# Projections and first layer in 64x32 tiles, scores and P V as separate visits, and a new order

## The chip, the cores and the metric

The kernel runs on one core of a Trainium2 chip. Its time is device microseconds of one execution; the median of several runs counts, and a profile shows one execution instruction by instruction. The core has TensorE (PE, matmuls; the loading of its stationary operand is listed apart as PEld), VectorE (DVE), ScalarE (ACT), GpSimd (POOL) and SyncE (SP), which here issues DMAs. [...]

## The reference

x is 2048 tokens by 448, bfloat16. Two branches start from its layer norm, and the result joins them:

```python
xn = _layernorm(x, axis=-1)
s = _A_ref(xn, A_wqkv, A_wo)
g = _silu(_B_ref(xn, B_w1, B_b1, B_w2, B_b2))
return x + s * g
```

Branch A is local attention with 16 heads of 28: every token attends to 8 keys, itself and those 2, 4, ... 14 tokens back.

```python
q, k, v = qkv[0], qkv[1], qkv[2]          # from xn @ wqkv
idx = pos[:, None] - off[None, :]         # off = 0, 2, ..., 14
logits = jnp.where(mask, einsum(q, kg) * Dh ** -0.5, -1e9)
o = einsum(softmax(logits), vg)           # then o @ wo
```

Branch B is a dense network: `gelu(xn @ w1 + b1) @ w2 + b2`, with w1 448 x 1792 and w2 1792 x 448.

## The kernel before

Tokens are put in the order "even ones first, then odd ones", so that the 8 keys of a token are 8 neighbours. There are 16 tiles of 128 tokens, in four chunks of 512, and nine attention blocks of 4 x 57 tokens (the fifth 4 x 56).

**Order.** Every piece of work is a task with engine, estimated cost, dependencies, buffers it takes and gives, and a priority (tables `PRIO` and `LATER`). `_Plan.run` plays the tasks through in time: of those that could start within `SLACK` (0.12 us) of the earliest on that engine, it takes the one of highest priority, with a bonus (`SAME` 20) for a TensorE task in the tile shape ("mode") that TensorE is in, and `TILED` 30 while it is in a small shape. A change of mode is booked at `SWITCH` 0.095 us. `emit` then issues all instructions in the order of planned starts, so each engine's program is fixed.

**TensorE's work.** The projections (`qk_rows` L532, `vproj` L556) and the first layer (`ff1` L591) have a contraction of 448 = 7 x 64. `pair` takes two such jobs, a and b, with a bank each: in four steps the upper 64 rows of the array serve a and the lower 64 serve b, then in three steps the other way round, so that all seven 64-row pieces of both are done in seven steps of two concurrent matmuls of 64x128 (`together`). Between the two parts a `nop` on GpSimd or SP waits for the last two matmuls of the first, and the first two of the second wait for the `nop` (`behind`), so that the two halves of the array never write one bank at once. `first_batch` does the first two tiles' projections in 128x128, with a last step in halves.

The second layer (`ff2_part` L627, 14 matmuls a tile) and the output projection (`final_part` L796, 4 a tile) use the whole array, 128x128. Scores (`scores_of` L677) use 32x64 tiles, 64 matmuls of 57 columns into four banks; P V (`values_of` L709) uses 64x32 tiles, 64 matmuls of 57 columns into two banks. `attn` makes visits of them: `VISITS` puts the scores of the first two blocks alone, then P V of block i together with the scores of block i+2 as one task.

**Other engines.** After scores, ScalarE takes the exponential of each of four banks (L687), and VectorE or GpSimd multiplies it by a 0/1 mask (L693; `MASK_ON` lets the planner choose, at 0.4 or 1.2 us). After P V, VectorE transposes, takes reciprocals, transposes back and scales (`output_of`, L719, L723, L728, L733). ScalarE does the GELU (L595) and the tanh of the second layer (L655); VectorE adds b2 (L649, y), forms g (L659), multiplies with the output projection (L801, sg) and adds x (L807, o; for the first eight tiles GpSimd may do it), and SP stores the tile (L811). The last tile is done in two halves of 224 columns. GpSimd's queue also issues the copies of v into windows (`dma_sb`, L354), and SP's the transposes of xn and of q, k (`dma_T`, L360) and the loads (L347). Exponentials and GELU are kept in stages (`STAGES`): GELU of chunks 0 and 1, exponentials of blocks 0 to 5, GELU of chunk 2, exponentials of blocks 6 to 8, GELU of chunk 3.

Of the kernel before, what the change touches and what calls it, by code (L numbers as in the profile page):

```python
# [17 lines left out]
TILED = 30  # L18
SAME = 20
HOPS = ("POOL", ("SP", "POOL"))  # L20
MASK_ON = (("DVE", "POOL"), (0.4, 1.2))


def VISITS(bs):
    out = [[("S", b)] for b in bs[:2]]
    for i, b in enumerate(bs):
        out.append([("P", b)] + [("S", c) for c in bs[i + 2:i + 3]])
    return out
# [11 lines left out]
class _Task:  # L40
    __slots__ = ("eng", "cost", "deps", "fn", "prio", "take", "give", "slots",
                 "start", "end", "on", "ndep", "users", "tail", "seq", "table", "limit", "mode", "out")


class _Plan:
# [7 lines left out]
    def add(self, eng, cost, fn, deps=(), prio=0, take=(), give=(), tail=0.0, table=(), limit=None,  # L53
            mode=128):
# [5 lines left out]
        t.mode, t.out = mode, None  # L60
# [14 lines left out]
    def _at(self, t, e, free):  # L75
        at = free.get(e, 0.0)
        for p, n in t.take.items():
            if len(p.free) < n or p.fifo and p.fifo[0] is not t:
                return None
            at = max(at, sorted(p.free)[n - 1][0] + HOP)  # L80
        if t.table and self.table not in t.table:
            at += TABLE
        for d in t.deps:
            at = max(at, d.end - d.tail if d.on == e else d.end + HOP)
        if e == "PE" and t.mode != self.mode:
            at = max(at, free.get(e, 0.0) + SWITCH)
        return at

    def run(self):
# [6 lines left out]
        self.mode = 128  # L96
        ready = [t for t in self.tasks if not t.ndep]
        order = []
        while ready:
# [14 lines left out]
            tiled = first[2] == "PE" and self.mode < 64  # L114
            at, t, e, c = min(near, key=lambda k: (-k[1].prio - (TILED if tiled and k[1].mode < 64 else SAME if k[2] == "PE" and k[1].mode == self.mode else 0),
# [4 lines left out]
            if e == "PE" and t.fn is not None:  # L120
                self.mode = t.out or t.mode
# [43 lines left out]
def kernel(  # L165
# [80 lines left out]
    def ring(name, n, shape, dt=BF16, fifo=False):  # L246
# [24 lines left out]
        "project": (49.5, 205, 104, 52.5,),  # L271
        "project2": (147, 150, 101, 61,),
        "values": (89.5, 62.5, 21, 58,),
        "attn": (185, 179.5, 78, 174.5, 106.5, 106, 138.5, 136.5, 32.5,),
        "ff1": (185, 180, 84.5, 176.5, 66.5, 64.5, 156.5, 189.5, 203, 146, 76, 114.5, 77.5, 179.5,
            75.5, 118.5, 180.5, 14.5, 163, 68, 151, 115.5, 194.5, 167.5, 180, 188.5, 86, 93,),
        "gelu": (62.5, 22.5, 95, 92.5,),
        "ff2": (144, 162.5, 103.5, 142.5, 44.5, 112.5, 67, 5, 89, 106.5, 101.5, 75, 74, 55, 11.5,
            6.5,),
        "final": (140, 19.5, 70.5, 47, 112, 34.5, 23.5, 142.5, 73, 53, 198.5, 188.5, 81.5, 126.5,  # L280
            180, 71,),
        "norm": (37.5, 132, 179.5, 129.5, 74.5, 99, 161, 69, 63, 62, 43.5, 73, -5.5, 90, 133.5,
            150,),
        "loads": (166.5, 166, 188, 139.5, 54.5,),
        "stats": (47.5, -60, 180.5, 23, 127, 56, 188.5, 77, 197.5, -13.5, 185, 205.5, 138, 14, 52.5,
            138.5,),
        "turn_x": (108.5, -1, 28, 116, 210, 116.5, 131.5, 160, 41.5, 79.5, 70, 119, -4.5, 74.5,
            132.5, 111,),
        "turn_qk": (68.5, 112, 174.5, 90, 80, 6, 149.5, 60.5, 4, 140.5, 199.5, 96.5, 103, 166.5,
            140, 156,),  # L290
        "move_v": (81.5, 95, 23, 95, 18.5, 26.5, 8, 128, 29.5,),
        "copies": (50, 119.5, 58.5, 76, 32.5, 135.5, 43, 1, 87, 79.5, 129, 77, 32, 41.5, 135,),
    }
    LATER = {"swap": 135, "qk": 165, "v": 29.5, "gelu": 30.5, "exp": 55.5, "mask": -60, "pv": 45, "recip": -16.5, "os": 54.5, "y": 153.5, "tanh": 182.5, "g": 58, "sg": 183, "o": 120.5}
# [50 lines left out]
    def dma(eng, dst, src, kb, prio, deps=(), issue=0.5, rate=350.0):  # L345
        def fn(_):
            {"SP": nc.sync, "ACT": nc.scalar, "POOL": nc.gpsimd}[eng].dma_start(dst, src)  # L347
        a = plan.add(eng, issue, fn, [t_on] + list(deps), prio)
        return plan.add("DMA", kb / rate, lambda _: None, [a], prio, tail=1.7)
# [16 lines left out]
    def load_x(t0, n, prio, eng="SP", deps=()):  # L366
        d = dma(eng, x_sb[:, t0:t0 + n, :],
                rows(x_half, t0 * P, n * P).rearrange("(t p) d -> p t d", p=P), 112 * n, prio, deps,
                rate=270.0 if t0 < TPC else 350.0)
# [11 lines left out]
    def load_w(kt, prio):  # L381
        t_w.append([dma("SP", w_in[:, kt, :], A_wqkv[kt * P:(kt + 1) * P, :], 336, prio, rate=270.0)])
# [6 lines left out]
    t_w.append([dma("SP", w_in3[:64], tails[:, 0:3:2, :], 112, PRIO["loads"][3], rate=270.0),  # L389
                dma("SP", w_in3[64:], tails[:, 1:3, :], 112, PRIO["loads"][3], rate=270.0)])  # L390
# [78 lines left out]

    def together(top, bottom):  # L470
        return [(f(), g()) for f, g in zip(top, bottom, strict=True)]
# [5 lines left out]
    def pair(a, b, prio, early=False):  # L477
# [11 lines left out]
        def f2(k):  # L489
            held["told"] = (nc.gpsimd if k.on == "POOL" else nc.sync).nop()  # L490
            for i in held["last"]:
                behind(held["told"], i)
        told = plan.add(HOPS[0] if early else HOPS[1], 0.06, f2, [t], 300)

        def f3(k):
            p, q = buf(p_b, t, 0), buf(p_b, t, 1)
            for i in together([part(b, q, kt, 0, kt + 4) for kt in range(3)], [part(a, p, kt, 1, kt + 4) for kt in range(3)])[0]:
                behind(i, held["told"])
# [5 lines left out]
    def first_batch(tiles, prio, tiles0=0):  # L504

        f = []
        for kt in range(3):
            for i, js in enumerate(tiles):
                def f1(k, kt=kt, i=i, js=js):
                    for q, j in enumerate(js):  # L510
                        j.part(buf(p_b, f[i] if kt else k, q), kt, 2, kt == 0, False)
# [14 lines left out]
    def qk_rows(t, which, prio):  # L526
        cs = slice(t * P, (t + 1) * P)

        def part(ps, kt, half, start, stop):
            r = half_rows(half)  # L530
            w = w_in[r, kt, which * D:(which + 1) * D] if kt < 3 else w_in3[r, 0, :]
            return nc.tensor.matmul(ps[:, :D], xnT[r, kt, cs], w, start=start, stop=stop)  # L532

        def evac(a, own, i):
# [6 lines left out]
            if len(t_row[t]) == 2:  # L541
                t_qk[t] = dma_T(qkT[:, :, :, cs].rearrange("p w g c -> p (w g) c"), lambda: b[:].rearrange("p w h c -> p (w h c)"),
                                t_row[t], PRIO["turn_qk"][t], None, 2, 1.9 if t < 3 else 3.8 if t == TPC else 2.0 if t == TPC + 1 else 1.27)
# [6 lines left out]
    def vproj(t, prio):  # L550
        k0 = t * P

        def part(ps, kt, half, start, stop):
            r = half_rows(half)
            w = w_in[r, kt, 2 * D:] if kt < 3 else w_in3[r, 1, :]
            return nc.tensor.matmul(ps[:, :D], xnT[r, kt, k0:k0 + P], w, start=start, stop=stop)  # L556
# [7 lines left out]
    def values(b):  # L564

        t_v[b], v_at[b] = [], []
        for i in range(2):
            first = None
            for w in range(2):
                k0 = VIS[b][2][w][i][1]  # L570
                for lo in sorted({k0, max(k0, (k0 + NK - 1) // P * P)}):
# [6 lines left out]
                    t_v[b].append(d)  # L578
# [6 lines left out]
    def ff1(c, mt, prio, gate):  # L585
# [3 lines left out]
        def part(ps, kt, half, start, stop):  # L589
            r = half_rows(half)  # L590
            return nc.tensor.matmul(ps[:], w1[r, kt, ms], xnT[r, kt, cs], start=start, stop=stop)  # L591
# [74 lines left out]
    def scores_of(b):  # L666
        q, nq, wins = VIS[b]

        def fn(banks):
            for i in range(2):  # L670
                for g in range(G):
                    for hl in range(4):
                        for w in range(2):
                            r = slice(32 * hl, 32 * hl + 32)
                            q0, k0 = wins[w][i]
                            c0 = (G * i + g) * nq
                            nc.tensor.matmul(banks[hl][NK * w:NK * w + NK, c0:c0 + nq], qkT[r, 1, g, k0:k0 + NK],  # L677
                                             qkT[r, 0, g, q0:q0 + nq], start=True, stop=True)
        return fn, [t_qk[t] for t in range(wins[0][0][1] // P, (q + 4 * nq - 1) // P + 1)]

    def weights_of(b, a, at, prio, gate):
# [3 lines left out]
        for hl in range(4):  # L685
            def f2(k, hl=hl):
                nc.scalar.activation(buf(p_E, k)[:, :n], buf(p_b, a, at + hl)[:, :n], ACT.Exp, scale=SCALE)  # L687
            e = plan.add("ACT", act(n), f2, [a] + gate, prio + LATER["exp"], take=(p_E,), give=((p_b, a, at + hl),), table=("exp",))
# [8 lines left out]
    def values_of(b, exps):  # L697
        nq = VIS[b][1]

        def fn(banks):  # L700
            for hl in range(4):
                E = buf(p_E, exps[hl])
                for i in range(2):
                    v = buf(*v_at[b][i])
                    for g in range(G):
                        for w in range(2):
                            r = slice(NK * w, NK * w + NK)
                            c0, c1 = (2 * hl + i) * nq, (G * i + g) * nq
                            nc.tensor.matmul(banks[w][32 * g:32 * g + 32, c0:c0 + nq], v[r, 4 * g + hl, :],  # L709
                                             E[r, c1:c1 + nq], start=True, stop=True)  # L710
        return fn, tuple((p_E, e, 0) for e in exps) + tuple(v_at[b])

    def output_of(b, po, i, w, prio):
# [4 lines left out]
        def f5(k):  # L718
            nc.vector.transpose(buf(p_dt, k)[:, :32 * m], buf(p_b, po, i)[:, :32 * m])  # L719
        d = plan.add("DVE", dve(32 * m), f5, [po], prio + LATER["recip"], take=(p_dt,))  # L720
# [11 lines left out]
        def f8(_):  # L732
            nc.vector.tensor_tensor(out=oT[:, :, q0:q0 + 2 * nq],  # L733
                                    in0=buf(p_b, po, i)[:, :n].rearrange("p (l q) -> p l q", l=4),
                                    in1=buf(p_dt, d)[:, :n].rearrange("p (l q) -> p l q", l=4), op=ALU.mult)
        o = plan.add("DVE", dve(n), f8, [rb], prio + LATER["os"], give=((p_b, po, i), (p_dt, d, 0)))
# [3 lines left out]
    last_visit = {"S": [], "P": []}  # L740
    state = {}

    def attn(b, what):

        deps, take, give, fns, cost = [], [], (), [], -SWITCH
        for n, (w, blk) in enumerate(what):
            if not n or what[n - 1][0] != w:
                cost += SWITCH
            cost += 0.215
            if not n:  # L750
                cost += 0.03
            at = len(take)
            if w == "S":
                fn, d = scores_of(blk)
                d = d + state["early"]
                take += [p_b] * 4
                fns.append(lambda k, fn=fn, at=at: fn([buf(p_b, k, at + i) for i in range(4)]))
            else:
                exps, masked = state[blk]
# [207 lines left out]
```

## Time and profile before

| what | value |
|---|---|
| median of 3 runs (lowest, highest) | 157.52 us (157.37, 158.0) |
| profiled execution: time; span of its instructions | 157.98 us; 156.2 us |
| L591, first layer: matmuls, busy | 392, 44.7 us |
| L532 and L556, projections | 318, 24.3 and 13.4 us |
| L627, second layer | 238, 45.2 us |
| L796, output projection | 68, 14.1 us |
| L677 and L709, scores and P V | 576 each, 6.9 and 6.2 us |
| L693, masks on GpSimd; on VectorE | 28, 30.8 us; 8, 3.0 us |
| PE instruction blocks fetched (queue q8) | 17, 0.28 MB |

"Busy" is the union of a group's spans. Matmuls overlap, so a group's busy time is not their number times their mean length, and the modelled end of a matmul lies some 0.15 us behind the moment when the next can begin. A place where TensorE's work passes from one line to another is best read in the chain of waits, which gives each microsecond to one line.

### The profile page before, as it was taken

What the parts mean: (1) busy time and instruction counts of PE and PEld (TensorE: products, weight loads), DVE (VectorE), ACT (ScalarE), POOL (GpSimd) and SP (SyncE); (2) the same over time, 40 slices, a digit from 0 to 9 for tenths busy, and PEclk for the clock granted to TensorE, in tenths of its full rate; (3) what the DMA queues carried; (4) which work ended last, traced back from release to release, by engine and by line L of the source; (5) the groups of instructions that cost most, each with busy time, mean ns of one, the idle gap of its engine ahead of it and who ended that gap; (6) DMA issues with size and microseconds to landing.
All of it is one profiled execution on the core that took longest, in us unless ns stands there. A gap on an engine that the chain in (4) does not pass through costs nothing.

```text
span 156.2 us, 5305 instructions
## 1 busy us (share of the span) xinstructions
PE 150.1 (96%) x2204; PEld 77.8 (50%) x2204; DVE 113.2 (72%) x259; ACT 83.3 (53%) x149; POOL 74.7 (48%) x123
## 2 busy tenths in 40 slices
PE   6999999999999999999999999999999999999980
PEld 2544454444455555455554644455556444545570
DVE  4789551486266758997799895109899996998992
ACT  3245867378889416444634149782496587051220
POOL 7854856000459408839261098389599780000000
PEclk9999999999999999999999999999999999999999
DMA  4999969999749443099039822123300100200211
GB/s 156 329 317 315 167 124 187 237 269 307 141 95 166 64 82 90 10 192 138 4 83 85 131 70 73 38 76 83 105 0 4 34 31 29 63 4 0 68 36 43
DMA packets 33575, 17.36 MB, mean 111 GB/s; under 512 B 25331, under 2 KB 32387, under 8 KB 33552
## 3 DMA queue, kind: packets, MB, share of 16 engines
q1 hardware_dynamic: 31472, 14.03, 41.3%
q0 software_dynamic: 1936, 2.88, 8.5%
q8 instruction: 17, 0.28, 0.8%
q10 hardware_dynamic: 144, 0.11, 0.2%
q14 instruction: 6, 0.05, 0.1%
HBM read 7.06 MB, written 1.84 MB: 57 GB/s over the span
## 4 chain that ended last, share of the span: by engine, by line
PE 80%; DVE 8%; DMA 3%; POOL 2%; issue 2%; ACT 1%; SPq 1%; DVEq 0%; ACTq 0%; POOLq 0%
PE bank L627 23%; PE bank L591 22%; PE bank L532 11%; PE bank L796 7%; PE bank L556 6%; PE bank L677 4%; PE bank L709 4%; PE bank L327 3%; DMA xnT<-xn 3%; POOL v L354 2%; DVE sg L801 2%; DVE o L807 1%; DVE w_in L659 1%; ACT E L687 1%; DVE xn L438 1%
## 5 line engine op out<-in xcount | busy, mean ns | idle before, releaser
L627 PE MATMUL bank<-w,h 128*128 128x448 bf16 (+1 forms) x238 | 45.2, 342 | 0.0
L591 PE MATMUL bank<-xnT,w 64*128 64x512 bf16 x392 | 44.7, 376 | 0.0
L595 ACT ACTIVATE h<-bank,b 128x512 bf16<-128x512 f32 x56 | 34.0, 689 | 12.9 <-PE bank L591 12.8
L354 POOL DMA_DIRECT2D v<-v_tok x52 | 27.6, 538 | 19.8 <-PE bank L709 9.0
L693 POOL TENSOR_TENSOR E<-E,m_gen 128x456 bf16<-128x456 bf16 x24 | 26.7, 1139 | 11.7 <-ACT E L687 9.5
L627 PEld LDWEIGHTS <-h 128*128 128x128 bf16 x238 | 22.3, 98 | 18.1 <-issue 0.4
L591 PEld LDWEIGHTS <-w 64*128 64x128 bf16 x392 | 19.1, 94 | 22.7 <-issue 1.1
L532 PE MATMUL bank<-w_in,xnT 64*128 64x448 bf16 (+1 forms) x212 | 24.3, 350 | 0.1
L687 ACT ACTIVATE E<-bank 128x456 bf16<-128x456 f32 (+1 forms) x36 | 17.0, 555 | 9.1 <-PE bank L677 9.1
L655 ACT ACTIVATE t<-y 128x448 f32<-128x448 f32 x15 | 8.7, 578 | 17.4 <-DVE y L649 17.4
L719 DVE STREAM_TRANSPOSE dt<-bank 128x480 f32<-128x480 f32 (+1 forms) x18 | 12.1, 671 | 5.6 <-PE bank L709 5.6
L532 PEld LDWEIGHTS <-xnT 64*128 64x128 bf16 (+1 forms) x212 | 10.6, 94 | 10.9 <-issue 1.1
L314 DVE CAST qk_tok<-bank 128x448 bf16<-128x448 f32 x16 | 9.4, 613 | 6.8 <-PE bank L532 6.8
L796 PE MATMUL bank<-wo,oT 128*128 128x448 bf16 (+1 forms) x68 | 14.1, 342 | 0.0
L312 ACT CAST qk_tok<-bank 128x448 bf16<-128x448 f32 x16 | 8.3, 533 | 10.6 <-PE bank L532 10.0
L556 PE MATMUL bank<-w_in,xnT 64*128 64x448 bf16 (+1 forms) x106 | 13.4, 349 | 0.0
L649 DVE TENSOR_TENSOR y<-bank,b 128x448 f32<-128x448 f32 x15 | 9.3, 620 | 4.9 <-PE bank L627 4.9
L728 DVE STREAM_TRANSPOSE dt<-rd 128x480 f32<-128x480 f32 (+1 forms) x18 | 12.1, 673 | 0.5
L733 DVE TENSOR_TENSOR oT<-bank,dt 128x456 bf16<-128x456 f32 (+1 forms) x18 | 11.3, 630 | 0.5
L404 DVE BATCH_NORM_STATS2 st<-x_sb 128x6 f32<-128x448 bf16 x16 | 9.6, 603 | 2.4 <-DMA x_sb<-in_A_x_dram 2.4
L438 DVE TENSOR_SCALAR xn<-x_sb,mv,rstd 128x448 bf16<-128x448 bf16 x16 | 6.3, 394 | 6.0 <-POOL rstd L426 5.8
L796 PEld LDWEIGHTS <-oT 128*128 128x128 bf16 x68 | 6.3, 98 | 6.3 <-issue 0.8
(62 smaller groups left out, 128.9 us busy)
## 6 DMA issues: line engine op xcount, KB each, us to landing
out_dram<-o SPq DMA_DIRECT2D x15, 112.0 KB, 1.7
w<-in_B_w_dram SPq DMA_DIRECT2D x2, 784.0 KB, 7.2
w<-in_B_w_dram SPq DMA_DIRECT2D x2, 672.0 KB, 7.0
x_sb<-in_A_x_dram SPq DMA_DIRECT2D x3, 448.0 KB, 6.3
v<-v_tok POOLq DMA_DIRECT2D x20, 64.0 KB, 2.5
w_in<-in_A_wqkv_dram SPq DMA_DIRECT2D x3, 336.0 KB, 4.3
w<-in_B_w_dram SPq DMA_DIRECT2D x4, 112.0 KB, 6.5
wo<-in_A_wo_dram POOLq DMA_DIRECT2D x4, 98.0 KB, 4.2
```

Of the source, the lines that this page charges most:

```text
L354: nc.gpsimd.dma_start(dst(k), src())
L532: return nc.tensor.matmul(ps[:, :D], xnT[r, kt, cs], w, start=start, stop=stop)
L556: return nc.tensor.matmul(ps[:, :D], xnT[r, kt, k0:k0 + P], w, start=start, stop=stop)
L591: return nc.tensor.matmul(ps[:], w1[r, kt, ms], xnT[r, kt, cs], start=start, stop=stop)
L595: nc.scalar.activation(buf(p_h, own, i)[:], buf(p_b, own, i)[:], ACT.Gelu_apprx_tanh, bias=b1[:, mt:mt + 1])
L627: nc.tensor.matmul(ps[:, :n], buf(*h_at[(c, mt)])[:, j * P:(j + 1) * P], w2[:, mt, cs], start=(mt == 0 and not biased), stop=(mt == NMT - 1))
L687: nc.scalar.activation(buf(p_E, k)[:, :n], buf(p_b, a, at + hl)[:, :n], ACT.Exp, scale=SCALE)
L693: (nc.gpsimd if k.on == "POOL" else nc.vector).tensor_tensor(out=E[:, :n], in0=E[:, :n], in1=m[:, :n], op=ALU.mult)
L719: nc.vector.transpose(buf(p_dt, k)[:, :32 * m], buf(p_b, po, i)[:, :32 * m])
L728: nc.vector.transpose(buf(p_dt, d)[:, :32 * m].rearrange("p (b c) -> p b c", c=32), buf(p_rd, r)[:, :m].unsqueeze(2).to_broadcast((P, m, 32)))
L733: nc.vector.tensor_tensor(out=oT[:, :, q0:q0 + 2 * nq], in0=buf(p_b, po, i)[:, :n].rearrange("p (l q) -> p l q", l=4), in1=buf(p_dt, d)[:, ...
L796: nc.tensor.matmul(ps[:, :n], oT[:, kt, t * P:(t + 1) * P], wo[:, kt, cs], start=(kt == 0), stop=(kt == KT - 1))
```

## The change

- `strips` splits each 64x128 matmul of projections and first layer into four 64x32 ones that write 32 partitions each of the same bank; `together` issues the eight of a step in turn, upper and lower rows alternately. The 128x128 steps of `first_batch` stay whole. The `nop` between the two parts of a pair waits for the last matmul alone, and only the first matmul after it waits for the `nop`.
- Scores and P V are tasks of their own (`visit`, `scores`, `attend`); P V's mode in the planner is now that of projections and first layer. A visit is booked at 0.5 us. `APART` books 0.25 us between two small visits in a row; `TILED` is gone.
- Masks are done by VectorE only. The output sum of tile 14 and of the first half of tile 15 is done by GpSimd only.
- The planner's figures for the first loads (rate 290 and tail 1.45 instead of 270 and 1.7) and for some transposes' issue are changed, and all of `PRIO` and `LATER` has new values. So the order is new on every engine. The loads' part of it:

```diff
-        "loads": (166.5, 166, 188, 139.5, 54.5,),
+        "loads": (137.5, 92.5, 134.5, 91.5, 23.5,),
-    LATER = {"swap": 135, "qk": 165, "v": 29.5, "gelu": 30.5, "exp": 55.5, "mask": -60, "pv": 45, "recip": -16.5, "os": 54.5, "y": 153.5, "tanh": 182.5, "g": 58, "sg": 183, "o": 120.5}
+    LATER = {"swap": 220, "qk": 0, "v": 65, "gelu": 121.5, "exp": 58, "mask": -4.5, "pv": 180, "recip": 48.5, "os": 77, "y": 146.5, "tanh": 71.5, "g": 91.5, "sg": 135, "o": 108}
```

With these, the second load of w_in is issued after the load of x tiles 2 and 3, not ahead of it. The rest of the diff, cut to its core:

```diff
-TILED = 30
+APART = 0.25
-MASK_ON = (("DVE", "POOL"), (0.4, 1.2))
+MASK_ON = ("DVE", 0.4)
...
+        if e == "PE" and t.thin and self.thin:
+            at = max(at, free.get(e, 0.0) + APART)
...
+    def strips(out, lhsT, rhs, half, start, stop):
+        n = P if half > 1 else 32
+        return [lambda c=c: nc.tensor.matmul(out[c:c + n], lhsT[:, c:c + n], rhs, start=start, stop=stop) for c in range(0, P, n)]
+
     def together(top, bottom):
-        return [(f(), g()) for f, g in zip(top, bottom, strict=True)]
+        done = []
+        for f, g in zip(top, bottom, strict=True):
+            done.append([q() for pair in zip(f(), g(), strict=True) for q in pair])
+        return done
...
-            for i in held["last"]:
-                behind(held["told"], i)
+            behind(held["told"], held["last"][-1])
...
-            for i in together([part(b, q, kt, 0, kt + 4) for kt in range(3)], [part(a, p, kt, 1, kt + 4) for kt in range(3)])[0]:
-                behind(i, held["told"])
+            behind(together([part(b, q, kt, 0, kt + 4) for kt in range(3)], [part(a, p, kt, 1, kt + 4) for kt in range(3)])[0][0], held["told"])
...
-            return nc.tensor.matmul(ps[:], w1[r, kt, ms], xnT[r, kt, cs], start=start, stop=stop)
+            return strips(ps[:], w1[r, kt, ms], xnT[r, kt, cs], half, start, stop)
...
+    def visit(what, fn, deps, prio, n, give):
         def f1(k):
-            for fn in fns:
-                fn(k)
+            for i in range(2):
+                fn([buf(p_b, k, j) for j in range(n)], i)
+        a = plan.add("PE", 0.5, f1, deps[0] + deps[1] + [last_visit[what]], prio, take=(p_b,) * n, give=give[0] + give[1], tail=0.15,
+                     mode=32 if what == "S" else 64, thin=True)
+        last_visit[what] = a
+        return a, a
...
-                for what in visits(run):
-                    exps += attn(what[0][1], what)
+                done = [(b, *scores(b, gels[:-1], gels)) for b in run]
+                for b, e, m in done:
+                    attend(b, e, m)
+                    exps += e
...
-        o = plan.add(("DVE", "POOL") if t < 2 * TPC else "DVE", (dve(n, 2), 1.15) if t < 2 * TPC else dve(n, 2), f3, [s], prio + LATER["o"], take=(p_o,), give=((p_sg, s, 0),))
+        o = plan.add("POOL" if t == NT - 2 or t == NT - 1 and not cs.start else ("DVE", "POOL") if t < 2 * TPC else "DVE",
+                     0.1 + n / 420 if t == NT - 2 or t == NT - 1 and not cs.start else (dve(n, 2), 1.15) if t < 2 * TPC else dve(n, 2), f3, [s], prio + LATER["o"], take=(p_o,), give=((p_sg, s, 0),))
```

## The prediction

> **What bounds the kernel now.** I read the page first (busy shares), then the chain of waits in order of time, then stretches of single matmul groups, then the last microseconds.
>
> ```profile
> PE 150.1 (96%) x2204; PEld 77.8 (50%) x2204; DVE 113.2 (72%) x259; ACT 83.3 (53%) x149; POOL 74.7 (48%) x123
> ...
> PE 80%; DVE 8%; DMA 3%; POOL 2%; issue 2%; ACT 1%; SPq 1%; DVEq 0%; ACTq 0%; POOLq 0%
> ```
>
> TensorE is busy from 5.6 us to 151.7 us: in stretches over that time its busy sum is 145.75 of 146.10 us, at granted clock 1.00. So from the first transposes to the last output projection the time is TensorE's own work, whatever the order. An edit pays only if it takes time out of TensorE, or out of the head (5.6 us) or the tail (from 151.7 to 156.2).
>
> What TensorE's time consists of, from the chain in order of time:
>
> ```profile
> 29.38 12.95 PE bank L591 x120
> ...
> 57.69 0.61 PE bank L709 x64
> 58.30 0.69 PE bank L677 x64
> 58.99 2.75 PE bank L627 x14
> ...
> 74.68 1.43 PE bank L627 x7
> ...
> 86.54 1.32 PE bank L627 x7
> ```
>
> First layer: 120 matmuls run two at a time, so 12.95 / 60 = 0.2158 us per slot (512 columns). The second layer takes 1.32 us for 7 after its own kind and 1.43 after another tile shape: a change of shape costs about 0.10 to 0.11 us. In the timeline I count 42 changes of shape, some 4.2 us. A visit of scores or of P V (64 small matmuls) takes 0.61 to 0.75 us with its change of shape.
>
> **The strips.** Each 64x128 matmul of projections and first layer becomes four 64x32 ones: 392 (L591) + 200 (L532) + 100 (L556) = 692 become 2768, with as many weight loads. Work per slot is the same columns, now as eight tiles instead of two, if three things hold: eight tiles stream at once, their weights load meanwhile, and the instructions arrive in time. P V already runs in this shape, so its trace can tell. Counts within a burst of one visit, then the same visit's second half:
>
> ```profile
> 57.60:57.65 0.05, 0.03 (x8) 0.03 (x9) 1.00 0.34 57
> 57.60:57.69 0.09, 0.06 (x16) 0.07 (x20) 1.00 0.32 43
> 57.60:57.71 0.11, 0.09 (x24) 0.09 (x28) 1.00 0.25 35
> 57.60:57.74 0.14, 0.12 (x32) 0.12 (x33) 1.00 0.21 28
> ```
> ```profile
> 57.84 0.45 PE L709 MATMUL bank<-E,v 64*32 64x57 bf16 x32
> ```
>
> (Columns of the first fence: stretch, its length, PE busy with the matmuls begun, PEld busy with the loads begun.) From 57.62 on 32 matmuls of 57 columns begin in 0.12 us, 8 per 0.03 us. The first layer's row gives 0.2158 us for 512 columns, so 57 columns take about 0.025 us: the eight tiles run side by side, and their loads keep pace. In the second half 32 begin in 0.45 - 0.19 (mean length of one) = 0.26 us, 8.3 ns each with its load: that is the feed once the queue has run dry. A slot's eight then need 0.067 us of feeding, against 0.189 (448 columns) or 0.216 us of streaming. So I cost a slot at **nothing more**; what hides loads and feed is the streaming of the slot before, and there are 196 + 150 = 346 slots. Bounds: below, 0, as the same columns stream; above, the first to the second eight of the burst begin about 0.04 us apart, 0.015 more than their columns take: if every slot showed that, 346 x 0.015 = 5.2 us. I take 0, as the third and fourth eight already come at 0.03.
>
> [...]
>
> **Changes of shape.** P V now has the shape of projections and first layer, so beside these it costs none; but scores are no longer joined to P V, where a joint visit needed three changes for two visits. Nine scores visits cost 18 changes; nine P V visits 0 to 18; the stretches of first layer and projections had some 18 and keep 12 to 18. That is 30 to 54 against 42: -1.2 to +1.2 us at 0.10. P V's priority is raised, which lets it break into second-layer work too, so I take the middle, 40: **-0.2 us**.
>
> **Scores apart.** Scores straight after P V took 0.69, 0.75, 0.63, 0.71 and 0.63 us, alone 0.63. With the two apart (the planner now holds small visits 0.25 us from each other, a choice of order and no wait) five excesses go: **-0.26 us**. The one idle spot of TensorE in this stage, 0.22 us before a scores matmul that waited for an exponential's bank, goes with shorter visits: **-0.22**, bound 0. The planner booked a visit at 0.245 us and now 0.5 plus the change; the trace's 0.61 agrees with the new figure, so planned times should miss less.
>
> **Masks to VectorE.** 28 of 36 masks leave GpSimd:
>
> ```profile
> L693 POOL TENSOR_TENSOR E<-E,m_gen x24: 1042/1048/1431, 51.2 to 127.0; 128x456 bf16<-128x456 bf16 x24
> L693 DVE TENSOR_TENSOR E<-E,m_gen x4: 385/388/391, 51.2 to 66.7; 128x456 bf16<-128x456 bf16 x4
> ...
> L659 DVE SCALAR_TENSOR_TENSOR w_in<-t,y x7: 615/1067/1464, 113.9 to 149.4; 128x448 bf16<-128x448 f32 x7
> ```
>
> VectorE gets 28 x 0.389 = 10.9 us more. It gets some back: line 659 takes 0.615 us undisturbed but 0.96 and 0.70 in the mean (7 and 8 of them), 3.0 us in excess, and the long ones lie beside GpSimd's masks; one output sum of 0.96 instead of 0.39 likewise. [...] So 113.2 + 10.9 - 3.5 - 0.7 (below) = 119.9 us of some 150: in stretches, VectorE had 43.6 of 60.0 us from 45 to 105, and 43.4 of 48.4 from 105 to 153.4. The last gets 12 masks, 4.7 us, and gives 2.4 + 0.7 back: 45.0 of 48.4. The cover is 3.4 us thin. I cost it at **0**; if the new order defers VectorE's work into that stretch, it is the bound (first rival). GpSimd loses 30.8 us of masks, and the v moves queued behind them issue sooner; nothing on the chain waits for them longer than it does now.
>
> **Tail.** From the end of the timeline:
>
> ```profile
> 150.78 0.39 DVE L807 TENSOR_TENSOR o<-x_sb,sg 128x448 bf16<-128x448 bf16 x1
> ...
> 152.00 0.28 DVE L807 TENSOR_TENSOR o<-x_sb,sg 128x224 bf16<-128x224 bf16 x1
> 152.19 0.38 DVE L659 SCALAR_TENSOR_TENSOR w_in<-t,bank 128x224 bf16<-128x224 f32 x1
> 152.68 0.39 DVE L801 SCALAR_TENSOR_TENSOR sg<-bank,w_in 128x224 bf16<-128x224 f32 x1
> 153.10 0.28 DVE L807 TENSOR_TENSOR o<-x_sb,sg 128x224 bf16<-128x224 bf16 x1
> ```
>
> VectorE's queue ends the program, 1.7 us behind TensorE. The output sums of tile 14 and of the first half of 15 (0.39 + 0.28) go to GpSimd, where the mask row prices them at about 1.04 and 0.5: both end near 152.4. The last output's issue comes after that of the half before it (0.33 us on SP), so of 0.67 I take **-0.6**, bounds 0 and -0.67.
>
> **Head, moved loads, hops.** w_in's second load issues behind the two x tiles on SP, one issue of 0.46 us and 224 KB later; it landed at 5.97 us and was not needed before 7.4, so 0. The hop between the two halves of a pair waits for one matmul, not two, and sits on a GpSimd with fewer masks: 0, as TensorE does not idle there now. The new priorities move nearly every instruction; each DMA stays on its queue (SP for loads, turns and outputs, POOL for v moves), and with TensorE full in any order I price the order at 0, between -1 and +3 us.
>
> **Sum.** 0 - 0.2 - 0.26 - 0.22 + 0 - 0.6 = -1.3 us. The profiled execution took 157.98 us (span 156.2 and 1.8 around it), 0.46 above the median of 157.52; so 156.7 in its own terms, and **156.2 us** in the median's.
>
> **Rivals.** (1) *VectorE becomes the bound of the last stage.* Place: from the last scores on. Each token tile whose second-layer end is deferred there adds 0.62 + 0.62 + 0.62 + 0.39 = 2.25 us (rows of lines 649, 659, 801, 807). With 3.4 us of cover it decides from the second tile on; three tiles make 6.75 - 3.4 = +3.4, so 157.5 + 3.4 - 0.5 = 160.4 us. For: VectorE is 90% busy there. Against: it idles 8.5 of 13 us from 92 to 105, which an order can use. (2) *Loads or feed of the strips show.* 346 x 0.015 = +5.2, less 1.3: 161.4 us. Against: the burst. For: PE's instructions come in 17 blocks (0.28 MB for 4408, so 64 B each and 256 a block); 256 would be used up in 16 slots, 3.3 us, where they lasted four times as long. (3) *Nothing gained*: P V breaks into second-layer work, 54 changes, +1.2 eats the rest: 157.4 us. (4) *P V melts in wholly*: 30 changes, -1.2, and 0.1 less for each visit with a full queue: 157.5 - 1.3 - 1.0 - 0.9 = 154.3 us.
>
> **Chances.** Forecast (155.2 to 157.0) 0.44, (4) 0.10, (3) 0.13, (1) 0.22, (2) 0.11. About 0.5% (0.8 us) is what a measurement can tell from none. Faster by more: most of the forecast and all of (4), 0.50; within: (3) and a little of the forecast, 0.16; slower: (1) and (2), 0.34. The range leaves out the far ends of (2) and (4): 154.6 to 160.6.
>
> **What would show it.** Right: L591 with about 1568 matmuls and a slot still 0.216 us in the chain; L709 at 0.5 us beside it; no POOL group on line 693; line 659 back near 0.62; VectorE's last op within 1.2 us of TensorE's. Wrong: slots of 0.23 and up, or idle TensorE released by PE's own queue (rival 2); TensorE idle behind banks that VectorE holds, or VectorE ending 3 us and more behind TensorE (rival 1).

## The result and the profile after

The changed kernel takes 182.81 us in the median of 4 runs (180.06 to 184.66), the kernel before 157.62. The ratio of the undisturbed runs is 1.1498 (95% interval 1.136 to 1.1635); two of the four runs of the changed kernel are not in it, so it lies below the quotient of the medians. The profiled execution, the shortest of the four, took 180.06 us; its span is 178.4 us, 22.2 us more than before.

From the page of the changed kernel (in the groups: count, busy us, mean ns, idle time before and its releaser):

```profile
PE 154.6 (87%) x4279; PEld 88.8 (50%) x4279; DVE 114.2 (64%) x275; ACT 87.1 (49%) x158; POOL 46.0 (26%) x98
...
PEclk9999999969999999999999999999999999999996
...
q8 instruction: 33, 0.54, 1.3%
...
PE 83%; issue 9%; DMA 3%; SPq 1%; DVE 1%; DVEq 0%
...
L467 PE MATMUL bank<-xnT,w 64*32 64x512 bf16 x1568 | 50.7, 383 | 5.9 <-issue 5.8
...
L467 PE MATMUL bank<-w_in,xnT 64*32 64x448 bf16 (+1 forms) x1218 | 39.6, 355 | 5.7 <-issue 5.6
```

Before, TensorE was without work for 0.35 of the 146 us of its main stretch. Now it idles before the strips (all on line 467 now) for 11.6 us, and no semaphore ends 11.4 of them ("issue"). P V waits in the same way for 3.4 us and the second layer for 0.7; together that is 17 waits and 15.5 us. 33 instruction blocks are fetched where 17 were. Where the waits lie shows the chain in order of time (start, length, what):

```profile
20.24 1.06 issue
21.30 3.65 PE bank L467 x128
24.95 0.36 issue
25.30 3.55 PE bank L467 x124
28.86 0.45 issue
29.31 3.41 PE bank L467 x128
32.71 1.97 issue
34.68 5.12 PE bank L467 x127
39.80 1.59 issue
41.39 3.65 PE bank L467 x128
45.04 0.35 issue
```

TensorE runs 128 matmuls (with their 128 loads of weights 256 instructions, one block: each of the 33 packets of q8 in the trace has 16384 bytes, and 0.54 MB over 4279 matmuls with a load each make some 64 bytes an instruction), then waits, then runs 128 again. (A count of 124 or 127 is a matter of records and of work booked to other lines.) While it runs, 128 strips of the first layer are 16 slots in 3.45 us or a little more: 0.216 us each, as before. So the array does what the prediction said, and the instructions do not arrive. The packets of the instruction queue stand in the trace beside the waits (us):

```
block begins   packet of the next   lands   next block begins
21.30          22.89                23.98   25.30
25.30          26.97                27.97   29.31
29.31          32.01                33.17   34.68
41.39          42.49                43.93   45.39
```

From the begin of one block to the begin of the next 4.0 us pass in the first, second and fourth row: 1.1 to 1.7 until the packet starts, 1.0 to 1.4 for the packet, 1.3 to 1.5 after it. Beside running loads the start is later: 1.6, 1.7 and 2.7 in the first three rows, at a DMA share of 1.08, 0.97 and 1.22 from the block's begin to the packet's start, against 1.1 at 0.09 in the fourth. Later in the run it also goes quicker: 3.45 us from 89.53 to 92.98 and 3.73 from 149.41 to 153.14. So 4.0 is a usual value and no lower bound.

Two more places. After the long wait at 32.7 the granted clock is low. Its mean is 0.64 over 4.7 us; read in parts it stays at 1.00 until 35.7, is 0.50 for the next 3.4 us and 1.00 again after that (stretch, length, busy and count of PE, PEld, DVE, ACT, POOL, clock, DMA share, GB/s):

```profile
29.30:32.40 3.10, 3.09 (x128) 2.03 (x128) 0.62 (x1) 1.94 (x5) 0.00 (x0) 1.00 1.24 242
34.70:39.40 4.70, 4.70 (x124) 2.69 (x128) 2.57 (x6) 1.06 (x2) 0.51 (x1) 0.64 1.29 272
35.70:39.10 3.40, 3.40 (x80) 1.83 (x72) 2.30 (x5) 1.06 (x2) 0.51 (x1) 0.50 1.24 241
```

And the end: VectorE's last instruction ends at 173.1 us, the span at 178.4. That is 5.3 us, where it was 2.8 before. What fills it are the closing instructions, read by their line, first after the change, then before it (duration min/median/max ns; first and last start):

```profile
L935 POOLq DRAIN  x3: 46/113/5468, 172.1 to 178.1; - x3
```
```profile
L962 POOLq DRAIN  x3: 46/92/4805, 135.8 to 155.9; - x3
```

GpSimd closes with a drain of some 5 us in both. Before, it began at 135.8 us, when GpSimd had nothing left to do, and was over long before the end. Now GpSimd's last output sum runs from 172.1 to 172.7 us and the drain is on record beside it from 172.1; it holds GpSimd until 177.5, that is 4.8 us after the sum's end, as long as before.

### The profile page after: what moved, and what is told of

It reads as the page before. It is cut to its first block, busy times and chain, and to the rows that moved or that the text cites. A ratio compares the mean times of both kernels' runs of the same rounds, so it can differ in the third digit from the quotient of the medians.

```text
span 178.4 us, 9431 instructions
## 1 busy us (share of the span) xinstructions
PE 154.6 (87%) x4279; PEld 88.8 (50%) x4279; DVE 114.2 (64%) x275; ACT 87.1 (49%) x158; POOL 46.0 (26%) x98
## 4 chain that ended last, share of the span: by engine, by line
PE 83%; issue 9%; DMA 3%; SPq 1%; DVE 1%; DVEq 0%
PE bank L467 44%; PE bank L627 24%; PE bank L770 7%; PE bank L707 4%; DMA w_in<-in_A_wqkv_dram 3%; PE bank L676 3%; SPq L342 1%; DVE sg L775 0%; PE bank L448 0%; DVE w_in L659 0%; DVE o L781 0%; PE bank L625 0%; PE bank L857 0%; DVEq L775 0%
## 5 line engine op out<-in xcount | busy, mean ns | idle before, releaser
L467 PE MATMUL bank<-xnT,w 64*32 64x512 bf16 x1568 | 50.7, 383 | 5.9 <-issue 5.8
L467 PE MATMUL bank<-w_in,xnT 64*32 64x448 bf16 (+1 forms) x1218 | 39.6, 355 | 5.7 <-issue 5.6
L467 PEld LDWEIGHTS <-w 64*32 64x32 bf16 x1568 | 26.3, 94 | 24.7 <-issue 11.4
L467 PEld LDWEIGHTS <-xnT 64*32 64x32 bf16 (+1 forms) x1218 | 21.3, 93 | 18.0 <-issue 9.2
L717 DVE STREAM_TRANSPOSE dt<-bank 128x480 f32<-128x480 f32 (+1 forms) x18 | 12.1, 674 | 12.3 <-PE bank L707 12.3
L307 ACT CAST qk_tok<-bank 128x448 bf16<-128x448 f32 x23 | 11.1, 542 | 13.5 <-issue 7.5
L309 DVE CAST qk_tok<-bank 128x448 bf16<-128x448 f32 x9 | 5.5, 619 | 17.7 <-PE bank L467 16.0
L781 POOL TENSOR_TENSOR o<-x_sb,sg 128x448 bf16<-128x448 bf16 (+1 forms) x3 | 2.8, 919 | 44.6 <-DVE sg L775 44.6
L692 DVE TENSOR_TENSOR E<-E,m_gen 128x456 bf16<-128x456 bf16 x28 | 10.9, 420 | 4.4 <-ACT E L686 4.3
L731 DVE TENSOR_TENSOR oT<-bank,dt 128x456 bf16<-128x456 f32 (+1 forms) x18 | 11.4, 631 | 0.6
L707 PE MATMUL bank<-E,v 64*32 64x57 bf16 (+1 forms) x576 | 7.7, 191 | 3.4 <-issue 3.4
L707 PEld LDWEIGHTS <-v 64*32 64x32 bf16 x576 | 6.5, 90 | 6.1 <-issue 4.8
```

Source lines behind the costliest of these rows:

```text
L307: nc.scalar.copy(o, i)
L467: return [lambda c=c: nc.tensor.matmul(out[c:c + n], lhsT[:, c:c + n], rhs, start=start, stop=stop) for c in range(0, P, n)]
L692: (nc.gpsimd if k.on == "POOL" else nc.vector).tensor_tensor(out=E[:, :n], in0=E[:, :n], in1=m[:, :n], op=ALU.mult)
L717: nc.vector.transpose(buf(p_dt, k)[:, :32 * m], buf(p_b, po, w)[:, :32 * m])
L731: nc.vector.tensor_tensor(out=oT[:, :, q0:q0 + 2 * nq], in0=buf(p_b, po, w)[:, :n].rearrange("p (l q) -> p l q", l=4), in1=buf(p_dt, d)[:, ...
```

## The experiments

**Strips undone: whole matmuls, everything else as changed.**

```diff
-        n = P if half > 1 else 32
+        n = P
```

> The changed kernel with its 64x128 matmuls whole again (order, visits, masks, sums as changed). Theory F (feed): TensorE's instructions arrive in blocks of 256; after a block begins, the next can begin some 4.0 us later at the earliest; the strips use a block up in 3.0 to 3.5 us and wait for the rest. With 2204 instead of 4279 matmuls the waits go: 158 us, between 156 and 160, no idle before TensorE over 0.5 us in total, clock 1.00. Rival C (column tiles stream or load weights slower): the same 158, so this run does not tell F from C. Rival O (the new order, the masks or the split visits cost the time): over 170 us.

158.86 us, ratio to the kernel before 1.0049 (1.0025 to 1.0072). No "issue" wait at a block's end is left. The strips account for all of the loss but some 0.8 us (the last output sums and the masks, tried alone below, are in these 0.8 with opposite signs); the rival "the order, the masks or the split visits" falls. The groups of line 467, with no idle time before them:

```profile
L467 PE MATMUL bank<-xnT,w 64*128 64x512 bf16 x392 | 45.3, 376 | 0.0
...
L467 PE MATMUL bank<-w_in,xnT 64*128 64x448 bf16 x300 | 31.6, 349 | 0.0
```

**Strips of 64x64.** Half the small matmuls, still column tiles.

```diff
-        n = P if half > 1 else 32
+        n = P if half > 1 else 64
```

> The changed kernel with two 64x64 matmuls in place of four 64x32. F: a block of 256 lasts 32 slots, 6 to 7 us, over the 4.0 us of the feed, so hardly a wait: within 1.5 us of the kernel with whole matmuls. C: still column tiles, with loads of 64 columns: half of the loss or more stays, 168 us and over, and a slot in the chain of waits is longer than 0.216 us. O: over 170 us.

159.17 us, ratio 1.0085 (1.0045 to 1.0126): 0.3 us above whole matmuls. The one idle time that its groups show, 0.6 us, ends with a transposed xn and not with an instruction block:

```profile
L467 PE MATMUL bank<-xnT,w 64*64 64x512 bf16 x784 | 45.6, 377 | 0.0
...
L467 PE MATMUL bank<-w_in,xnT 64*64 64x448 bf16 x600 | 31.8, 350 | 0.6 <-DMA xnT<-xn 0.6
```

So column tiles of 64 cost nothing that shows, and twice the instructions cost nothing, as a block of 256 then lasts 32 slots, an estimated 6 to 7 us (32 x 0.189 to 0.216).

**The old kernel and order, with strips alone.** `strips`, the new `together` and the single hop of the change, put into the kernel before.

```diff
-        return [(f(), g()) for f, g in zip(top, bottom, strict=True)]
+            done.append([q() for pair in zip(f(), g(), strict=True) for q in pair])
...
-            return nc.tensor.matmul(ps[:], w1[r, kt, ms], xnT[r, kt, cs], start=start, stop=stop)
+            return strips(ps[:], w1[r, kt, ms], xnT[r, kt, cs], half, start, stop)
```

> The kernel before, in its own order, with only the strips (four 64x32 in place of each 64x128). F: 12 blocks of first layer lose some 0.5 us each and 9 of projections 1.0 us each, more while the loads run, and the clock drops in the gaps: 172 to 180 us, idle before TensorE of 12 us and more at multiples of 256 instructions. C: the same time, but as longer slots and not as gaps. O: 158 us, no gaps.

178.47 us in one run, 20.4 over the kernel before. Idle time before the strips is 10.1 us, and scores and P V now wait for blocks too (3.2 and 1.3 us), since a boundary can fall into them:

```profile
L472 PE MATMUL bank<-xnT,w 64*32 64x512 bf16 x1568 | 50.0, 397 | 4.1 <-issue 4.1
...
L472 PE MATMUL bank<-w_in,xnT 64*32 64x448 bf16 x1200 | 32.7, 350 | 6.0 <-issue 5.8
...
L682 PE MATMUL bank<-qkT 32*64 32x57 bf16 x512 | 6.4, 199 | 3.4 <-issue 3.2 <-ACT E L692 0.2
```

**Four times the instructions without column tiles.** In the old kernel, each 64x128 matmul is split along its moving columns; stationary operands stay 128 columns wide.

```diff
+        n = rhs.shape[-1] if half > 1 else rhs.shape[-1] // 4
+        return [lambda c=c: nc.tensor.matmul(out[:, c:c + n], lhsT, rhs[:, c:c + n], start=start and not c, stop=stop and c + n == rhs.shape[-1]) for c in range(0, rhs.shape[-1], n)]
```

> The kernel before with each 64x128 matmul of projections and first layer split in four along the moving columns (112 or 128 each): four times the instructions as in the change, but no column tiles and stationary operands of the full 128 columns. F: gaps at block boundaries as with the strips, at least 10 us of idle before TensorE released by nothing the profile shows, 170 us and over (loads of weights may add to it as longer slots). C: no gaps at block boundaries; without a limit of the weight loads 158 us.

174.64 us in one run. The same rhythm of 128 matmuls and a wait, without a column tile on this line (chain in order of time):

```profile
20.06 2.15 issue
22.21 3.63 PE bank L472 x128
25.84 0.10 issue
```

This separates the number of instructions from the tile shape. The number it is; the shape costs nothing that can be seen. The run with strips took 3.8 us longer than this one, but not on the line itself: in the chain line 472 has 45.9% of 176.6 us there and 46.9% of 172.8 here, 81 us both times, and the waits have 9.4% and 7.6%, 16.6 and 13.1 us. Both are single runs.

**Strips in one of the two alone,** on the fast version below: 1200 in the projections, then 1568 in the first layer.

```diff
-        n = P
+        n = P if half > 1 or rhs.shape[-1] == CH else 32
```

> The fast version (whole matmuls, sums on VectorE, 156.5 us) with strips in the projections alone: 1200 matmuls in place of 300. F: a block of 256 instructions is used up in 16 slots of 0.189 us, 3.0 us, and the next needs 4.0: at most 9 blocks x 1.0 us, less where other work between lets the feed catch up: 159 to 166 us, gaps at block boundaries inside the projections only. A cost that goes with the number of small matmuls (1200 of 2768, of some 22 us): 166 us, spread evenly.

```diff
-        n = P
+        n = 32 if half < 2 and rhs.shape[-1] == CH else P
```

> The same with strips in the first layer alone: 1568 matmuls in place of 392. F: a block lasts 16 slots of 0.216 us, 3.45 us, and waits up to 0.55: 12 blocks, 6.7 us at most where the loads are over, more while they run: 160 to 167 us, and no more than with the projections although there are more matmuls. A cost by number: 169 us. Under F the two losses together stay under the 22 us of both at once, as whole matmuls in between let a block arrive.

167.47 us (ratio 1.0603, 1.0447 to 1.0759) and 166.86 us (1.0564, 1.0393 to 1.0735). That is 11.0 and 10.4 us over the 156.48 without strips (10.8 and 10.2 by the ratios). The first layer, with 1568 against 1200 matmuls, does not lose more, as the feed has it. With two runs each and intervals of some 2.5 us to either side, the times alone do not exclude a price by number (166 and 169 us); the chains do, as the loss is not spread evenly. The projections lose more than I allowed (159 to 166), the first layer lies at the upper end of its range. The two losses make 21.4 us, near that of both together, although the waits without a releaser do not: 4.2% of 166.5 and 3.9% of 165.9 us, less 0.6 each, are 12.3 us against 15.4 with both split. So whole matmuls in between do let blocks arrive, as expected, and other things fill the sum. The chain of the projections' run, and below it the stretch after its long wait (columns as above), show one:

```profile
18.28 14.96 PE bank L467 x256
33.23 2.61 issue
35.84 17.91 PE bank L467 x294
...
84.51 0.62 PE bank L707 x64
85.12 0.53 issue
85.66 3.22 PE bank L467 x128
88.88 0.23 issue
```
```profile
35.85:39.50 3.65, 3.65 (x44) 1.33 (x46) 2.44 (x5) 1.06 (x2) 0.51 (x1) 0.59 1.09 375
```

One long wait while the large loads run (2.61 us), after which the clock stands at 0.59 in the mean of 3.65 us, costs some 4 us at once. One wait of this kind occurs in either kernel, whichever of the two is split (3.16 us from 38.51 in the other), so it is counted twice in the sum. Another is the mixture itself: by the matmuls' shapes in the traces, TensorE changes shape 57 and 55 times in these runs and 43 times in the version without strips, which at the prediction's 0.10 us is an estimated 1.2 to 1.4 us of each loss.

**The last output sums.** The kernel with whole matmuls, and these sums on VectorE at the same places:

```diff
-            eng = nc.gpsimd if k.on == "POOL" else nc.vector
+            eng = nc.gpsimd if k.on == "POOL" and t < NT - 2 else nc.vector
```

> The changed kernel with whole 64x128 matmuls, and the last output sums (tile 14, first half of 15) on VectorE again. Theory D (drain): a sum on GpSimd within the last microseconds makes GpSimd's closing drain last 5.5 us and hold the end; without it the span ends 2.8 us after VectorE's last instruction, as before the change, and not 5.3: 156.8 us, between 156 and 157.3, some 2 us under the kernel with whole matmuls alone. Rival: the sums on GpSimd save VectorE 0.6 us as predicted, and the long end has another cause: 159.4 us.

156.48 us, ratio 0.992 (0.989 to 0.9949): 2.0 us by the ratios (2.4 by the medians, which come from two chips) under the run that differs in this alone, and faster than the kernel before. The reverse, the sums put on GpSimd in the kernel before:

```diff
+            eng = nc.gpsimd if k.on == "POOL" or t == NT - 2 or t == NT - 1 and not cs.start else nc.vector
```

> The kernel before with only those last sums moved to GpSimd. D: VectorE ends 0.4 to 0.7 us sooner, but the drain on GpSimd lasts 5 us and more and the whole takes 1.5 to 2.5 us longer: 159.8 us. Rival (as predicted): 0.6 us shorter, 157.5.

159.86 us, ratio 1.0117 (1.0097 to 1.0136). VectorE ended sooner (152.76 against 153.38 us) as predicted, and the program 1.9 us later. The drain in the kernel with the sums on VectorE, then in the old one with them on GpSimd:

```profile
L935 POOLq DRAIN  x3: 46/107/4805, 133.4 to 154.2; - x3
```
```profile
L962 POOLq DRAIN  x3: 46/98/5482, 151.7 to 157.7; - x3
```

Here too the drain ends 4.8 us after the last sum (152.3 to 157.2 us).

**The loads in the old order,** on the version with whole matmuls and VectorE's sums.

```diff
+    x23.fn, w_2.fn = w_2.fn, x23.fn          # the two issues change places
```

> As the run with whole matmuls and VectorE's sums, with the second and third 1st-stage loads issued in the old order (the piece of w_in ahead of the two x tiles). Theory H: the wait for w_in that the chain shows at 8.6 to 9.3 us comes from that order, and the head gains 0.4 to 0.7 us: 156.2. Rival: the landing at 8.3 to 9.3 us is spread between executions (the old order's own runs show 7.9 to 8.5): within 0.3 us of the run without it.

156.71 us, ratio 0.9914 (0.989 to 0.9937), against 156.48 and 0.992: no difference. The piece of w_in that the head waits for landed at 7.6 us here and at 8.8 without, but in kernels with the old order anywhere from 7.9 to 8.8; the order of these loads is not worth anything that these runs can tell.

**All masks on VectorE,** in the kernel before.

```diff
-                (nc.gpsimd if k.on == "POOL" else nc.vector).tensor_tensor(out=E[:, :n], in0=E[:, :n], in1=m[:, :n], op=ALU.mult)
+                nc.vector.tensor_tensor(out=E[:, :n], in0=E[:, :n], in1=m[:, :n], op=ALU.mult)
```

> The kernel before with all masks on VectorE, at the planned places. As predicted: line 659 falls to 0.62 us each, VectorE's busy time rises from 113.2 to 120.6 us, and the time stays within 1 us, as TensorE has other work: 158. Rival (VectorE becomes the bound of the last stage): 160 us and over, VectorE's last instruction more than 3 us behind TensorE's.

156.81 us, ratio 0.9929 (0.9907 to 0.9952). Faster, not merely equal. VectorE is busy for 116.4 us, 3.2 more than before and not 7.4, and line 659 is back at its undisturbed length:

```profile
L659 DVE SCALAR_TENSOR_TENSOR w_in<-t,y x7: 556/614/626, 114.1 to 149.1; 128x448 bf16<-128x448 f32 x7
```

Where TensorE gains, its timeline and ScalarE's show. In the kernel before, ScalarE loads its table for the exponentials (1.28 us) only after the scores, and TensorE's next visit of scores is held up by the exponentials that follow:

```profile
111.52 1.28 ACT L687 ACT_TABLE_LOAD   x1 [5.00 <-PE bank L677]
...
112.81 0.55 ACT L687 ACTIVATE E<-bank 128x456 bf16<-128x456 f32 x1
...
114.76 0.65 PE L677 MATMUL bank<-qkT 32*64 32x57 bf16 x58 [0.22 <-ACT E L687]
```

With the masks on VectorE the table is loaded in the idle time before, and the visit runs through:

```profile
106.85 1.28 ACT L687 ACT_TABLE_LOAD   x1
...
111.80 0.55 ACT L687 ACTIVATE E<-bank 128x456 bf16<-128x456 f32 x1 [3.66 <-PE bank L677]
...
114.46 0.70 PE L677 MATMUL bank<-qkT 32*64 32x57 bf16 x64
```

From the visit before this one to the end of this one the chain takes 4.59 us before and 4.02 here, so some 0.6 of the 1.2 us lies at this place. Why the load waits for the scores in one kernel and not in the other, and where the rest lies, no run isolates.

## Why the prediction was wrong

The forecast was 156.2 us, with 154.6 to 160.6; the kernel takes 182.81. Faster was the wrong side. (The chance given to slower, 0.34, is 0.33 by its two parts.)

**The strips: the step that failed.** "A slot's eight then need 0.067 us of feeding, against 0.189 or 0.216 us of streaming. So I cost a slot at nothing more" was wrong. That feed rate was read from visits of 128 instructions, half a block; it is the rate at which instructions leave a block that is there, not the rate at which blocks come. Two of the three conditions held (eight tiles stream at once, weights load meanwhile: slots of 0.216 us after the change, and the 64x64 run). The third did not: 16 instructions per slot use up 256 in 3.0 to 3.45 us, and the next block mostly takes 4.0 and more. The upper bound of 5.2 us was priced for exposed weights, and so missed this cost. Against the fast version (whole matmuls, sums on VectorE, span 154.4 us) the 24.0 us that the profiled execution loses are made up so: waits without a releaser 9.0% of 178.4 less 0.4% of 154.4, 15.4 us; line 467 in the chain 44.3% of 178.4 less 47.9% of 154.4, 5.1 us (about 1.7 of it the low clock, 0.36 x 4.7; the rest, by its place, the last matmul's way out before each wait: 17 waits at some 0.17, a strip's length less its slot, are an estimated 2.9 us, which no run isolates); P V 0.5; the end behind VectorE 5.3 less 2.5, 2.8 us. Together 23.8.

**The rival that came true, mis-sized.** Rival 2 named the mechanism in its second half (256 used up in 16 slots, 3.3 us) but took its price from the first half, 0.015 us a slot; right would have been a block's round trip less its use, times 22 blocks. With 4.0 us that is 0.55 for first-layer blocks and 1.0 for projections, some 16 us, close to the 15.4 measured as waits. That it is so close is partly luck: block by block the trace shows 17 waits of 0.2 to 2.2 us in the place of 22 of 0.55 or 1.0. The profile before does not show the 4.0: there no block was used up fast enough. Small transfers of 1.6 to 4.8 us from issue to landing in its table of DMA issues were the nearest rows, and would have opened the range upward.

**The tile shape** has no price here: neither the strips' slots (128 strips of the projections take 3.22 us in the chain, 16 slots of 0.189 and the last one's way out) nor the 64x64 run (159.17 us against 158.86 with whole matmuls) show one. What bore on the case is the supply of instructions. The waits shown stand behind 128 pairs of matmul and weight load, and the next packet starts 1.1 us and more after a block begins; with TensorE using a block up in 3.0 to 3.45 us, against a round trip of mostly 4.0 and more, it comes too late.

**Tail: wrong sign.** In the old order VectorE did end sooner, as the step said (0.6 us in the reverse run); in the new order it ends 1.2 us behind TensorE's last matmul with the sums on GpSimd and 1.1 with them on VectorE, so there was next to nothing to gain. What I left out is what queues behind the moved instruction on GpSimd: its closing drain of about 5 us. Moving the sums cost 1.9 us in the old order (157.99 to 159.86) and 2.0 to 2.4 in the new one instead of gaining 0.6.

**Masks: VectorE right, the time not.** "I cost it at 0" should have been about -1.2 us (157.99 to 156.81, the single edit). That "the time is TensorE's own work, whatever the order" passed over one place: the chain goes through ScalarE from 111.5 to 114.8 us. The 0.22 us of idle time there, which I put down to the joint visits, stood for some 0.6 us, and these went with GpSimd's masks alone, with the visits as before. Line 659 fell to 0.62 us as said, but VectorE's busy time is 116.4 us in that run, not 120.6, and 114.2 after the change, not 119.9 (there the new order also gives 9 of its 23 casts to ScalarE); rival 1 (VectorE as bound) did not appear in any run.

**Changes of shape, split visits, head, order:** -0.7 us together was predicted. The version with whole matmuls and VectorE's sums gains 1.5 us on the kernel before (157.99 to 156.48), and the masks' own run has 1.2 of that, so some 0.3 is left for the order and the split visits, no more than the intervals leave open. P V shares no shape with the rest in that version. In the changed kernel the trace has 29 changes of shape where 42 were; I took 40, and rival 4 had 30. At 0.10 us that is an estimated 1.3 us, hidden under the waits, and no run isolates it.

## What to carry to other kernels

Instructions are a supply with a rate of their own: here one block of 256 in 3.45 to 4.0 us at best, 64 to 74 per us, some 14 to 16 ns each, and longer beside large loads (5.4 us from 29.31 to 34.68), however fast a short burst runs (8.3 ns for a matmul with its load in P V's visit before the change). Before splitting a matmul, divide 256 by the instructions per slot and compare the time of that many slots with a block's round trip: 4 and 8 instructions a slot were free (158.86 and 159.17 us), 16 cost 15 us of waits in 22 blocks. And an engine's last instruction is not its end: GpSimd's closing drain took 4.8 us after its last work in the kernels read here, and in both orders it set the end when that work lay in VectorE's last microseconds.

## What the runs showed of the hardware that was not expected

- In the changed kernel TensorE stopped 17 times, for 0.2 to 2.2 us, where a block of 256 instructions was used up and the next had not come; it began again 1.3 to 1.8 us after the block's packet landed, most often 1.3 to 1.5.
- With some waits of 2 to 3 us came a lower granted clock, 0.50 for 3.4 us, so that such a wait costs up to 1.7 us more than its length. In the five kernels with waits at block ends (mean granted clock of the profiled executions 0.975 to 0.989, against 1.000 for the kernel before) it came with six of them (1.97, 2.52, 2.61, 2.79, 3.04 and 3.16 us), beginning from 0.4 us before the wait's end to 1.2 us after it, and not with three others (2.15, 2.19 and 2.33 us). What decides between them no run isolates.
- GpSimd's closing drain lasted 4.8 us (4805 ns) where it began at 135.8 us, in the kernel before, and at 133.4, in the fast version. Where its record shows 5.5 us (5468 and 5482 ns), it begins beside the last output sum, which still runs for 0.6 to 0.7 of them.
- A mask on GpSimd lengthens line 659 on VectorE from 0.62 to as much as 1.46 us; without GpSimd's masks all 17 of its instructions on whole tiles with y as input into w_in (7 in the masks' run, 5 each in the changed kernel and in the fast version) lie at 0.63 us or below.
